# Strassen's scheme for the gate and value products of the last 832 tokens, with its weight sums made on the chip

## The chip, the cores and the metric

The kernel runs on one core of one Trainium2 chip. The metric is the device time of one execution in microseconds (us); the time of a kernel is the median of its runs. A profiled execution gives the trace; its span runs from the first instruction to the last.

## What is computed

Attention with a forget bias over 4 x 8 heads of 576 positions and head size 64, then a gated layer and a second layer, all in fp32:

```python
x = attention(q, k, v, s)                  # 2304 tokens x 512
g = x @ w_gate                             # 512 x 1536
x = (g * sigmoid(g) * (x @ w_val)) @ w_out # 1536 x 512
h = x @ w_in                               # 512 x 2048
out = (h * sigmoid(h)) @ w_out2            # 2048 x 512
```

## The kernel before

Every fp32 product is made of three matmuls: an operand is split into a high part that TensorE takes as fp32r and a low part (the rest), and high x high, high x low and low x high are added in PSUM. "Cutting" a tile means a copy on ScalarE that makes the high part and a subtraction, on POOL or VectorE, that makes the low part.

The first layer goes over three token groups of 576, 896 and 832 tokens (`SIZE`), called group zero, one and two here. Each group goes through the nine chunks of `L1`: two gate chunks, a down chunk, and so on three times. A gate chunk ("gv") holds 256 columns of the gate and of the value weights; `gate` makes, for each of two column blocks and each half of the tokens, two PSUM banks of 12 matmuls each, and `silu_mul` turns them into one tile of `h`. A down chunk ("o1") takes the last four tiles of `h`; `down` makes eight steps of 12 matmuls, and each is added into `acc` from PSUM. The weights of a chunk come in two loads of 1 MB (`w_half`, L416), the high and the low part side by side, asked for when the chunk before begins; `wt_p` has four such buffers, two chunks.

Attention runs beside group zero (its first units before it) and group one. The x of group two is written to DRAM as attention makes it and read back in the last chunk of group one (`x3_load`, `x3_cut`, L604 to L612).

The second layer (`up2`, `down2`) multiplies by Strassen's scheme in Winograd's form, with seven products in place of eight. Its weights need sums and cuts, which are prepared ahead, in 16 sets, beside the first layer. One set is: two loads of raw 64-bit weights, 512 KB each and in two DMAs (`ahead_load`, L457); their unpacking, two operations on ScalarE and two on VectorE for each load (`ahead`, `unpack`, L428 to L439); four sums on POOL (`u_sum`, L486); a cut of the weights themselves, 768 columns, and one of the sums, 1024 columns (`u_cut`, L497); and four stores to DRAM (`u_store`, L506). All these buffers come from `raw_p`, which has five. Eight sets are prepared beside group one, at every third or fourth quarter of a chunk, and eight beside group two, one in each of its first eight chunks. The x of the second layer's first 768 tokens is cut into its seven operands beside chunks one to seven of group two (`x2_sub`, `x2_cut`).

In group one the order on ScalarE, VectorE, POOL and SP comes from a planner that simulates the timeline, and only TensorE's is written by hand. From the last chunk of group one on (`last`, L949) every engine works in the order of the program: all queues are in order, SP, which issues the DMAs, among them. In that loop L991 to L1003 the functions of `more[n]` follow a quarter of a chunk's matmuls, stores of a set are put behind the next quarter's functions (`late`), and `after` holds the loads of the next set.

Of the kernel before, what the change touches and what calls it, by code (L numbers as in the profile page):

```python
# [33 lines left out]
BASE = [0, S, 2 * S + 320]  # L34
NG = len(SIZE)
# [38 lines left out]
def kernel(  # L74
# [13 lines left out]
    second_layer = ctx.enter_context(ExitStack())  # L88

# [314 lines left out]
    def w_load(c):  # L404
        wst[c] = []
        g = place[stream[c]]
        if first[c]:
            for e in range(CW // DW):
                t = raw_p.tile([P, DW, 2], U32, tag="wraw", name="r64")
                nc.sync.dma_start(out=t, in_=w64[g, :, e * DW : (e + 1) * DW, :])  # L410
                wst[c].append(t)
            return
        for e in range(2):
            w_half(c, e)
# [133 lines left out]
    def silu_mul(t, ph, hi, lo, n, pg, pv):  # L548
        u = tmp_p.tile([P, max(SIZE) // 2], F32, tag="u", name="u")[:, :n]
        if t == NG - 1:  # L550
            nc.scalar.activation(out=u, in_=pg[:, :n], func=AF.Silu)  # L551
        else:
            nc.scalar.activation(out=u, in_=pg[:, :n], func=AF.Tanh, scale=0.5)
            nc.vector.scalar_tensor_tensor(out=u, in0=u, scalar=1.0, in1=pg[:, :n], op0=ALU.add, op1=ALU.mult)  # L554
# [18 lines left out]
    def down(c, g, m, n0, n):  # L573
        b = batch[c]
        ps = ps_m.tile([P, 512], F32, tag="m", name="po")
# [28 lines left out]
    def x3_load(g):  # L604
        r = p2["x3", g] = raw_p.tile([P, SIZE[2]], F32, tag="wraw", name="x3r")
        nc.sync.dma_start(out=r, in_=x3_d[g])

    def x3_cut(g):
        r = p2.pop(("x3", g))
        x = xin[2][g] = p2["xt"].tile([P, 2, SIZE[2]], F32R, tag="x3", name="x3")  # L610
        copy("a", x[:, 0], r)
        nc.vector.tensor_tensor(out=x[:, 1], in0=r, in1=x[:, 0].bitcast(F32), op=ALU.subtract)  # L612

    def x2_load(t):
        for i in range(2):
            r = p2["x2", i] = p2["x2r"].tile([P, 2, 2, TN], F32, tag="x2r", name="x2r")
# [238 lines left out]
    def body():  # L855
# [47 lines left out]
        for q in range(8):  # L903
            x = 1 + 7 * q // 2
            for e in range(2):
                at_quarter(7 * (q - 1) // 2 + 2 if q else x - 4, lambda i=2 * q + e: ahead_load(i))
                at_quarter(x + e, lambda i=2 * q + e: ahead(i))
# [35 lines left out]
        p2["xt"] = pool("x3", NP, scope=first_layer)  # L943
        p2["x2"] = pool("x2", 10, scope=second_layer, side="right")
        p2["x2r"] = pool("x2r", 2, scope=second_layer, side="right")
        p2["ps"] = pool("ps_o", 4, PS, scope=second_layer, side="right")
        stores = []
        g = nc.gpsimd
        for c in range(last, n1):  # L949
            cur = chunk_steps(c)  # L950
            k = c - last - 1
            more = [[] for _ in range(4)]
            extra = []
            if k < 0:
                for x in range(NP):
                    more[0].append(lambda x=x: x3_load(x))
                    more[2 + x // 2].append(lambda x=x: x3_cut(x))
            if c + 1 < n1:
                more[0] += [lambda e=e: w_half(c + 1, e) for e in range(2)]
            q = 8 + k  # L960
            if 0 <= k < 8:
                more[0].append(lambda q=q: ahead(2 * q))
                more[1] += [lambda q=q: ahead(2 * q + 1), lambda q=q: u_sum(q)]
                for e in range(2):
                    more[2 + e].append(lambda q=q, k=e: u_cut(q, k))
                    more[2 + e].append(
                        lambda q=q, k=e: stores.extend(lambda e=e: u_store(q, k, e) for e in range(2))
                    )
            after = [[] for _ in range(4)]
            if k < 7:  # L970
                after[3].append(lambda i=2 * q + 2: ahead_load(i))
            if 0 <= k < 8:
                after[0].append(lambda i=2 * q + 1: ahead_load(i))
            if k == 0:
                more[2].append(lambda: x2_load(0))
            sub = {1: 1, 2: 2, 4: 3, 5: 4}.get(k)
            cuts = {1: [0], 2: [1], 3: [2, 3], 4: [4], 5: [5], 6: [6]}.get(k, [])
            if sub:
                more[0].append(lambda: x2_sub(0, sub))
            for e, x in enumerate(cuts):  # L980
                src = None if x in (0, 2, 5) else {1: 1, 3: 2, 4: 3, 6: 4}[x]
                f = lambda x=x, src=src: x2_cut(0, x, None if src is None else p2["t", src], g)
                if len(cur) == 4:
                    more[2].append(f)
                else:
                    extra.append(f)
            if k == 7:
                more[3].append(lambda: u_load(1, "Z"))
            if k == 8:
                more[0].append(lambda: u_load(0, "ZS"))  # L990
            for n, stp in enumerate(cur):  # L991
                if n == 0:
                    wst.pop(c - 1, None)
                stp()
                todo = more[n] if len(cur) == 4 else more[n // 2] if n % 2 == 0 else extra[n // 4 : n // 4 + n // 2 % 2]
                late, stores[:] = list(stores), []
                for f in todo:
# [106 lines left out]
```

## Time and profile before

| | |
|---|---|
| median of 3 runs | 1059.21 us (1057.55 to 1059.47) |
| profiled execution | 1057.37 us |
| its span | 1055.5 us |
| TensorE busy | 1010.6 us, 96% of the span |
| VectorE, ScalarE, POOL busy | 53%, 50%, 55% |
| mean granted TensorE clock | 0.983 |
| DMA | 254.87 MB, mean 241 GB/s |

The span has three parts that matter here: up to 492 us attention and the groups zero and one, to 699 us group two, and to the end the second layer. TensorE is the engine that is nearly always busy; matmuls are pipelined, so a row's time for one matmul is longer than the distance from one start to the next, and the rate is read from the starts. In rows, PE is TensorE, DVE is VectorE, ACT is ScalarE, SPq the queue that issues DMAs; L120 is the helper `copy`. The granted clock is a share of full speed. A line of windows ends with the mean granted clock, the DMA engines' busy share and GB/s.

### The profile page before, as it was taken

What the parts mean: (1) busy time and instruction counts of PE and PEld (TensorE: products, weight loads), DVE (VectorE), ACT (ScalarE), POOL (GpSimd) and SP (SyncE); (2) the same over time, 40 slices, a digit from 0 to 9 for tenths busy, and PEclk for the clock granted to TensorE, in tenths of its full rate; (3) what the DMA queues carried; (4) which work ended last, traced back from release to release, by engine and by line L of the source; (5) the groups of instructions that cost most, each with busy time, mean ns of one, the idle gap of its engine ahead of it and who ended that gap; (6) DMA issues with size and microseconds to landing.
All of it is one profiled execution on the core that took longest, in us unless ns stands there. A gap on an engine that the chain in (4) does not pass through costs nothing. (4 is left out here: it accounts for less than half of the span.)

```text
span 1055.5 us, 17759 instructions
## 1 busy us (share of the span) xinstructions
PE 1010.6 (96%) x6128; PEld 930.9 (88%) x6128; DVE 554.4 (53%) x1363; ACT 526.1 (50%) x1242; POOL 583.2 (55%) x729
## 2 busy tenths in 40 slices
PE   8999999999999999999978779799999999999998
PEld 7788878888888888889978769799999999999998
DVE  5877656655553554524211232236667666666556
ACT  6879877874475564422333423323345445443333
POOL 4766656553675776520444544534478555674445
PEclk9999999999999999999988989999999999999999
DMA  8479865888686855538755555699667977676663
GB/s 234 140 237 321 271 232 190 281 274 280 204 273 218 301 199 185 185 130 292 267 213 190 189 202 192 220 350 358 236 229 284 348 279 279 236 296 259 235 232 120
DMA packets 84138, 254.87 MB, mean 241 GB/s; under 512 B 10640, under 2 KB 33680, under 8 KB 70992
## 3 DMA queue, kind: packets, MB, share of 16 engines
q1 hardware_dynamic: 83904, 253.54, 67.7%
q8 instruction: 48, 0.79, 0.3%
q14 instruction: 42, 0.34, 0.1%
q10 hardware_dynamic: 144, 0.20, 0.1%
HBM read 194.26 MB, written 59.45 MB: 240 GB/s over the span
## 5 line engine op out<-in xcount | busy, mean ns | idle before, releaser
L672 POOL TENSOR_TENSOR h<-u,h 128x384 fp32r<-128x384 f32 x72 | 74.9, 1040 | 144.7 <-ACT h L120 137.1
L544 PE MATMUL pgv<-xt,wt 128*128 128x288 f32 (+1 forms) x384 | 131.5, 342 | 4.9 <-DVE u L554 4.9
L544 PE MATMUL po<-h,wt 128*128 128x288 f32 (+2 forms) x288 | 103.7, 360 | 27.2 <-ACT u L551 14.3
L557 POOL TENSOR_TENSOR h<-u,h 128x288 fp32r<-128x288 f32 (+2 forms) x72 | 74.0, 1029 | 99.0 <-ACT h L120 99.0
L545 PE MATMUL pgv<-xt,wt 128*128 128x288 f32 (+1 forms) x384 | 128.1, 334 | 0.0
L546 PE MATMUL pgv<-xt,wt 128*128 128x288 f32 (+1 forms) x384 | 127.9, 333 | 0.0
L120 ACT ACTIVATE h<-u 128x384 fp32r<-128x384 f32 (+3 forms) x144 | 75.0, 521 | 92.5 <-DVE u L555 91.6
L740 PE MATMUL po<-h,wt 128*128 128x384 f32 x336 | 112.5, 335 | 0.0
L741 PE MATMUL po<-h,wt 128*128 128x384 f32 x336 | 112.4, 335 | 0.0
L742 PE MATMUL po<-h,wt 128*128 128x384 f32 x336 | 112.4, 334 | 0.0
L695 PE MATMUL pu<-x,wt 128*128 128x384 f32 x330 | 111.8, 339 | 0.0
L698 PE MATMUL pu<-x,wt 128*128 128x384 f32 x330 | 111.8, 339 | 0.0
L699 PE MATMUL pu<-x,wt 128*128 128x384 f32 x330 | 111.8, 339 | 0.0
L672 POOL TENSOR_TENSOR h<-t,h 128x384 fp32r<-128x384 f32 x96 | 107.0, 1136 | 5.5 <-ACT h L120 5.5
L276 ACT ACTIVATE e<-e,m 64x64 f32<-64x64 f32 (+4 forms) x160 | 88.4, 553 | 34.6 <-DVE m L263 33.9
L545 PE MATMUL po<-h,wt 128*128 128x288 f32 (+2 forms) x288 | 101.1, 351 | 0.0
L546 PE MATMUL po<-h,wt 128*128 128x288 f32 (+2 forms) x288 | 100.6, 349 | 0.0
L701 ACT ACTIVATE s<-pu 128x384 f32<-128x384 f32 x48 | 23.6, 492 | 153.4 <-PE pu L699 153.4
L751 DVE TENSOR_TENSOR acc<-po,acc 128x384 f32<-128x384 f32 x144 | 76.8, 558 | 36.3 <-PE po L742 35.6
L124 POOL TENSOR_SCALAR e<-e,rl 128x128 f32<-128x128 f32 (+3 forms) x128 | 68.5, 548 | 43.2 <-DVE rl L288 41.9
L434 DVE SCALAR_TENSOR_TENSOR dk<-z,dk 128x512 uint32<-128x512 uint32 x32 | 26.8, 838 | 124.4 <-ACT dk L432 121.1
L544 PEld LDWEIGHTS po<-h,wt 128*128 128x128 f32 x288 | 57.1, 198 | 36.2 <-ACT u L551 15.3
(122 smaller groups left out, 2543.6 us busy)
## 6 DMA issues: line engine op xcount, KB each, us to landing
wt<-wu_d SPq DMA_DIRECT2D x48, 1024.0 KB, 8.6
wt<-w_d SPq DMA_DIRECT2D x36, 1024.0 KB, 7.4
wt<-wu_d SPq DMA_DIRECT2D x47, 768.0 KB, 5.9
r<-in_w_dram SPq DMA_DIRECT2D x36, 512.0 KB, 5.9
w_d<-wt SPq DMA_DIRECT2D x18, 1024.0 KB, 7.3
r<-in_w_dram SPq DMA_DIRECT2D x64, 256.0 KB, 4.9
qkr<-in_qk_dram SPq DMA_DIRECT2D x32, 288.0 KB, 5.3
cumb<-cum_d SPq DMA_DIRECT2D x15, 576.0 KB, 6.1
```

What stands on the lines that cost most here:

```text
L276: nc.scalar.activation(out=e[:r, hd, :wd], in_=e[:r, hd, :wd], func=AF.Exp, bias=m[hd][:r], scale=-1.0, accum_out=l[:r, hd : hd + 1],)
L544: nc.tensor.matmul(out=ps[:, :n], lhsT=a, rhs=xh, start=(k == 0), stop=False)
L545: nc.tensor.matmul(out=ps[:, :n], lhsT=a, rhs=xl, start=False, stop=False)
L546: nc.tensor.matmul(out=ps[:, :n], lhsT=c, rhs=xh, start=False, stop=(k == last))
L672: nc.gpsimd.tensor_tensor(out=h[:, 1], in0=u, in1=h[:, 0].bitcast(F32), op=ALU.subtract)
L695: nc.tensor.matmul(out=o, lhsT=a, rhs=x[:, 0, kk], start=fresh and kk == 0, stop=False, skip_group_check=True)
L698: nc.tensor.matmul(out=o, lhsT=a, rhs=x[:, 1, kk], stop=False, **more)
L699: nc.tensor.matmul(out=o, lhsT=c, rhs=x[:, 0, kk], stop=kk == 1, **more)
L740: nc.tensor.matmul(out=ps, lhsT=a, rhs=h[:, 0], start=fresh, stop=False, skip_group_check=True)
L741: nc.tensor.matmul(out=ps, lhsT=a, rhs=h[:, 1], stop=False, **more)
L742: nc.tensor.matmul(out=ps, lhsT=c, rhs=h[:, 0], stop=e == 1, **more)
L751: nc.vector.tensor_tensor(out=o, in0=ps, in1=o, op=ALU.add)
```

## The change

Group two's gate and value products go by the same seven-product scheme as the second layer: `up1` takes the place of `gate` there, over blocks of 256 features, 128 columns and `HN` = 416 tokens. For each chunk it makes seven products of six matmuls for the gate (`e` = 0) and seven for the value (`e` = 1), 84 matmuls of 416 columns. The products are added on VectorE, in PSUM or SBUF, the silu is taken by ScalarE from PSUM, and product, copy and low half give the tiles of `h`.

The sums of the weights are made beside the products, for each half chunk: `s_join` adds the high and low part of a weight load back together (1024 columns), `s_sum` makes four sums of 256, both on VectorE, and `s_cut` cuts them on ScalarE and POOL. The operands of x are cut by a new `x3_cut` from four differences (`x3_sub`), five of seven in the last chunk of group one.

Eleven sets are prepared beside group one in place of eight, three quarters of a chunk apart, from a quarter of the chunk ahead of it on. The other five go beside chunks two to six of group two. In these chunks the order is a table of positions: `fill[c, pos]` holds what follows product `pos` (of 14) of a gate chunk or step `pos` (of 8) of a down chunk. Down steps of group two take their PSUM banks from the pool `ps_o`, which also serves the unpacking. All seven cuts of the second layer's first x, and its first weight loads, move into the last down chunk.

```diff
 SIZE = [S, S + 320, 2 * S - 320]
+HN = SIZE[2] // 2
+NAHEAD = 11
...
     def down(c, g, m, n0, n):
         b = batch[c]
-        ps = ps_m.tile([P, 512], F32, tag="m", name="po")
+        if "ps" in p2:
+            ps = p2["ps"].tile([P, 512], F32, tag="o", name="po")
+        else:
+            ps = ps_m.tile([P, 512], F32, tag="m", name="po")
...
+    def x3_cut(i, eng):
+        x = p2["x3", "x", i] = p2["xm"].tile([P, 2, 2, HN], F32R, tag="x3", name="x3")
...
+        copy("a", x[:, 0], src)
+        eng.tensor_tensor(out=x[:, 1], in0=src, in1=x[:, 0].bitcast(F32), op=ALU.subtract)
+
+    def s_join(c, e):
+        z = p2["s", c, e, "z"] = p2["zs"].tile([P, CW // 2], F32, tag="zs", name="zs")
+        hi, lo = [x.bitcast(F32) for x in wst[c][e]]
+        nc.vector.tensor_tensor(out=z, in0=hi, in1=lo, op=ALU.add)
+
+    def s_sum(c, e):
...
+            nc.vector.tensor_tensor(out=o, in0=a, in1=b, op=op)
+
+    def s_cut(c, e):
+        r = p2["s", c, e, "r"]
+        t = p2["s", c, e] = p2["sp"].tile([P, 2, CW // 2], F32R, tag="sp", name="sp")
+        copy("a", t[:, 0], r)
+        nc.gpsimd.tensor_tensor(out=t[:, 1], in0=r, in1=t[:, 0].bitcast(F32), op=ALU.subtract)
+
+    def up1(c, e, fill):
...
+            u = g[j]
+            v.tensor_tensor(out=u, in0=x, in1=u, op=ALU.mult)
...
+            copy("a", hi, u)
+            nc.gpsimd.tensor_tensor(out=lo, in0=u, in1=hi.bitcast(F32), op=ALU.subtract)
+
+        for pos, (name, k, xi, bank) in enumerate(UP):
...
+            if xi in (0, 1):
+                y = ps["s", xi] = part(f"s{xi}")
+                nc.scalar.activation(out=y, in_=o, func=AF.Copy)
+            if xi == 3:
+                ps["w"] = part("w")
+                add(ps["w"], o, ps["s", 0])
+            if xi == 4:
+                add(o, o, ps["w"])
...
+                add(g[3] if e == 0 else ps["s", 1], o, ps["s", 1])
+            if xi == 2:
+                done(0, o)
+                done(3, g[3] if e == 0 else ps["s", 1])
+            if xi == 5:
+                add(o, o, ps["w"])
+                done(1, o)
+            if xi == 6:
+                done(2, o)
+            for f in fill.get((c, e * 7 + pos), []):
+                f()
...
-        for q in range(8):
-            x = 1 + 7 * q // 2
+        for q in range(NAHEAD):
+            x = 3 * q - 3
             for e in range(2):
-                at_quarter(7 * (q - 1) // 2 + 2 if q else x - 4, lambda i=2 * q + e: ahead_load(i))
+                at_quarter(x - 2, lambda i=2 * q + e: ahead_load(i))
...
+        def ahead_all(q, k, a0, a1, a2, a3, a4, a5, a6):
+            c = last + 1 + k
+            size = {"gv": 14, "o1": 8}
+            at(c - 1, size[stream[c - 1][0]] * 3 // 4, lambda: ahead_load(2 * q))
+            at(c, 0, lambda: ahead_load(2 * q + 1))
+            at(c, a0, lambda: ahead(2 * q))
+            at(c, a1, lambda: ahead(2 * q + 1))
+            at(c, a2, lambda: u_sum(q))
+            for k, pos in ((0, (a3, a4)), (1, (a5, a6))):
+                at(c, pos[0], lambda k=k: u_cut(q, k))
+                at(c, pos[1], *[lambda k=k, e=e: u_store(q, k, e) for e in range(2)])
...
+        for c in range(last, n1 - 1):
+            at(c, 0, *[lambda c=c, e=e: w_half(c + 1, e) for e in range(2)])
+        at(last, 2, lambda: x3_cut(0, g))
+        at(last, 3, lambda: x3_sub(1), lambda: x3_sub(2))
+        at(last, 4, lambda: x3_cut(3, v))
+        at(last, 5, lambda: x3_cut(1, g))
+        at(last, 6, lambda: x3_sub(3), lambda: x3_cut(4, v))
+        at(last, 7, lambda: x3_cut(2, g), lambda: x3_sub(4))
+        at(c0, 0, lambda: x3_cut(5, v))
+        at(c0, 1, lambda: x3_cut(6, g))
+        for c in range(c0, n1):
+            if stream[c][0] == "gv":
+                if c == c0:
+                    s_make(c, 0, last, 4, 5, 6)
+                elif stream[c - 1][0] == "gv":
+                    s_make(c, 0, c - 1, 7, 8, 9)
+                else:
+                    s_make(c, 0, c - 1, 4, 5, 6)
+                s_make(c, 1, c, 0, 1, 2)
+        for q in range(NAHEAD, 2 * NPR):
+            k = q - NAHEAD + 1
+            pos = (2, 6, 7, 9, 11, 11, 13) if stream[c0 + k][0] == "gv" else (1, 3, 4, 5, 6, 6, 7)
+            ahead_all(q, k, *pos)
+        at(c0 + 3, 0, lambda: x2_load(0))
...
+                at(c, 0, lambda: u_load(0, "ZS"), lambda: u_load(1, "Z"), sub(1), cut(0, g))
+                at(c, 1, sub(2), cut(3))
+                at(c, 2, cut(1, g))
+                at(c, 3, sub(3), cut(4))
+                at(c, 4, cut(2, g))
+                at(c, 5, sub(4), cut(5))
+                at(c, 6, cut(6, g))
```

## Rows read from the trace of the kernel before

**Rows 1.** Windows: us, then busy us (x instructions) of PE, PEld, DVE, ACT, POOL.

```profile
260.00:492.10 232.10, 232.10 (x1357) 196.46 (x1356) 110.18 (x302) 115.98 (x274) 128.98 (x180) 1.00 0.65 222
492.10:698.80 206.70, 176.06 (x865) 169.94 (x865) 47.99 (x77) 66.01 (x112) 94.10 (x79) 0.93 0.60 219
698.80:1055.50 356.70, 353.26 (x2018) 352.93 (x2016) 223.40 (x377) 150.24 (x326) 205.90 (x182) 1.00 0.69 265
```

**Rows 2.** Timeline of PE: start us, us, engine, line, operation, tiles.

```profile
252.60 0.37 PE L544 MATMUL pgv<-xt,wt 128*128 128x448 f32 x1
...
492.12 0.35 PE L544 MATMUL pgv<-x,wt 128*128 128x416 f32 x1
...
528.15 0.34 PE L546 MATMUL pgv<-x,wt 128*128 128x416 f32 x1
532.64 0.72 PE L544 MATMUL po<-h,wt 128*128 128x416 f32 x1 [4.14 <-ACT u L551]
...
538.95 0.35 PE L544 MATMUL po<-h,wt 128*128 128x416 f32 x1
```

**Rows 3.** Waits in group two: who for whom, us in total, times, longest.

```profile
PE po L544 <- ACT u L551: 14.3, 3, 5.8
...
ACT z L431 <- DMA r<-in_w_dram: 81.1, 15, 8.8
```

**Rows 4.** Timeline of SP's queue in group two: set loads (L473, L466), weight loads (L418).

```profile
495.40 1.07 SPq L473 DMA_DIRECT2D r<-in_w_dram  x2
...
641.45 1.01 SPq L418 DMA_DIRECT2D wt<-w_d  x2
642.56 0.90 SPq L473 DMA_DIRECT2D r<-in_w_dram  x2
...
667.01 1.34 SPq L466 DMA_DIRECT2D r<-in_w_dram  x2
```

**Rows 5.** Timeline of ACT: the unpack that waited for the load of 642.56.

```profile
652.81 0.66 ACT L431 ACTIVATE z<-r 128x512 f32<-128x512 f32 x1 [4.40 <-DMA r<-in_w_dram]
```

**Rows 6.** Timeline of POOL for the same set: first of four sums, low halves.

```profile
655.57 0.73 POOL L495 TENSOR_TENSOR s<-z 128x256 f32<-128x256 f32 x1 [6.00 <-DVE z L437]
...
659.51 1.85 POOL L503 TENSOR_TENSOR z<-z,cut 128x768 fp32r<-128x768 f32 x1
661.31 1.86 POOL L628 TENSOR_TENSOR x<-tt,x 128x768 fp32r<-128x768 f32 x1
...
664.16 2.40 POOL L503 TENSOR_TENSOR s<-s,cut 128x1024 fp32r<-128x1024 f32 x1
```

**Rows 7.** Groups by form in group two: count, busy us, mean ns, idle before.

```profile
L557 POOL TENSOR_TENSOR h<-u,h 128x416 fp32r<-128x416 f32 x24 | 26.1, 1089 | 53.8 <-ACT h L120 53.8
...
L555 DVE TENSOR_TENSOR u<-pgv,u 128x416 f32<-128x416 f32 x24 | 14.1, 588 | 38.3 <-PE pgv L546 22.1 <-ACT u L551 16.2
L120 ACT ACTIVATE h<-u 128x416 fp32r<-128x416 f32 x24 | 13.2, 552 | 34.1 <-DVE u L555 34.1
...
L586 DVE SCALAR_TENSOR_TENSOR acc<-po,acc 128x416 f32<-128x416 f32 x16 | 9.1, 588 | 14.5 <-PE po L546 14.3
```

**Rows 8.** Timeline of SP's queue in group one: loads of three sets.

```profile
260.24 2.80 SPq L466 DMA_DIRECT2D r<-in_w_dram  x4
...
295.37 2.69 SPq L473 DMA_DIRECT2D r<-in_w_dram  x4
...
314.05 5.99 SPq L466 DMA_DIRECT2D r<-in_w_dram  x4
```

**Rows 9.** Group by form: a subtraction of 832 elements on DVE.

```profile
L612 DVE TENSOR_TENSOR x<-x3r,x 128x832 fp32r<-128x832 f32 x4 | 3.9, 1017 | 0.0
```

**Rows 10.** Tile t of the second layer: count, ns min/median/max, first and last start.

```profile
L672 POOL TENSOR_TENSOR h<-t,h x96: 1002/1022/1344, 708.5 to 1044.5; 128x384 fp32r<-128x384 f32 x96
L677 DVE TENSOR_TENSOR t<-u,t x48: 810/925/1194, 707.4 to 1039.6; 128x384 f32<-128x384 f32 x48
...
L720 DVE TENSOR_TENSOR t<-u,pu x24: 543/544/546, 707.0 to 1038.1; 128x384 f32<-128x384 f32 x24
```

## Prediction: what the change does to the time

> **What bounds the kernel now.** I read the stages first: one line for the stretch from token group one's own chunks to its end, one for group two, one for the second layer [rows 1]. TensorE is busy all of the first stretch and nearly all of the last at the full clock; group two is the exception, 176.06 of 206.7 us busy at a mean clock of 0.93. So 30.6 us of idle time lie in the very stage that the change rewrites, and more time is lost to the low clock level.
>
> Next, how fast TensorE could go there. The 192 gate and value matmuls of the first two chunks start at 492.12 and the last of them at 528.15 [rows 2]: 36.03 us over 191 intervals, 0.1886 us each. The stage has 576 of these and 288 in the three down chunks: 864 x 0.1886 = 162.9 us against 206.7, 43.8 us lost. The same rows show how it is lost: 4.14 us of idle before the first down matmul, and then 18 matmuls from 532.64 to 538.95, 0.35 us each, which is the 1.2 GHz level; at the other level they would take 3.4 us, so 2.9 us more go.
>
> Then who is waited for. TensorE waits for ScalarE's silu, and ScalarE itself waits 81.1 us, 15 times, for one kind of transfer: the raw second-layer weights that the sets prepare ahead [rows 3]. ScalarE works in order, so an unpack whose data has not landed holds the silu behind it. The sync queue shows why the data is late. The last load of a set goes out at 495.40 for the first set and at 667.01 for the eighth [rows 4]: 171.61 / 7 = 24.5 us a set, while a chunk needs 96 x 0.1886 = 18.1 us. **The sets, not the matmuls, pace eight of the nine chunks.** One turn of that loop: landed 652.81 [rows 5], sums start 655.57, first low half 659.51, an x2 low half 661.31, second low half 664.16 to 666.56 [rows 6]; then its store, and at once the next load at 667.01 [rows 4]. That is 14.2 us to the load, and 10.25 us from the load at 642.56 to its landing at 652.81.
>
> **Part by part.**
>
> *Fewer products.* Seven of eight: per chunk 2 x 42 = 84 matmuls for 96, 72 fewer in six chunks, 72 x 0.1886 = 13.6 us of TensorE time; the stage's floor goes to 792 x 0.1886 = 149.4 us. It counts in full only in the chunks that no set paces: the first, and the fifth and sixth gate chunks.
>
> *Five sets instead of eight in group two*, in chunks two to six of nine. The loop's turn is built again. Landing to sums 2.8 us, the four sums 2.9, first low half 1.85, second 2.4. The x2 low half (1.86) leaves; in a gate chunk two low halves of h at 1.09 each [rows 7] come between: 12.1 us. On the sync queue the store now goes first, then the two weight loads, then the set's load. From the first weight load at 641.45 [rows 4] to the landing at 652.81 [rows 5] it is 11.36 us, and the store ahead of it adds 0.45 (666.56 to 667.01): 11.8 us. Turn: 23.9. In the down chunk a weight cut of 2.4 replaces the halves: 24.1, and I take 24.5 because its ScalarE part waits for a step's evacuation. In the third gate chunk the cut comes on top: 12.1 + 2.4 + some 1.2 for the join on VectorE ahead of it + 11.8 = 27.5. Four turns lie between the first and the fifth set: 24 + 24.5 + 27.5 + 24 = 100, plus 1.5 for operations of VectorE and POOL that hold each other up (below): 101.5. The queue's order matters: the store of a set's sums waits for POOL, and behind it wait both halves of the next chunk's weights, on SP and so on VectorE, which joins their two parts.
>
> *The sum.* First chunk from 492.1 to 507.9 (84 x 0.1886 = 15.8). The weight loads behind it wait for its buffers; the set's load follows 1.1 us later (641.45 to 642.56) and lands 10.25 after [rows 4, 5]: 519.2. Fifth landing 519.2 + 101.5 = 620.7. The down chunk beside it then has about four of eight steps left, 4 x 12 x 0.1886 = 9.1: 629.8. Two free gate chunks 31.7: 661.5. Before the last down chunk the final low half of h is late: product 0.59, copy 0.55, POOL 1.09 and one more in its queue 1.09 [rows 7], 3.3 in all, against 10 matmuls, 1.9, that need not wait: 1.4. The chunk itself 18.1: 681.0, where 698.8 stood. **17.8 us less.** The profiled execution took 1057.4 us, so 1039.6; it stands 1.8 below the median of the three runs, so about **1041** against 1059.2.
>
> *Three more sets in group one*: no TensorE work. Each brings 4 loads and 4 stores on SP, four unpacks, four decodes, four sums on POOL, two cuts. POOL takes 7.2 us a set: 21 us more on 129 busy of 232 [rows 1]. Spacing falls from 23 to about 20 us (three quarters of a chunk; group one's 36 quarters take 492.1 - 252.6 = 239.5 us, [rows 2]). TensorE never idles there now, and a spacing of 18.7 us occurs, 295.37 to 314.05 [rows 8]. I take 0; the other end is rival C.
>
> *Preparing x*: five of seven cuts and four differences move into the down chunk ahead of group two, beside 96 matmuls of 448 columns, 19.5 us (18.1 x 448 / 416). A subtraction of 832 elements takes 1.02 on VectorE [rows 9]; POOL by its rows about 2. VectorE: four differences, two low halves, eight evacuations at 0.59 [rows 7], one join and its sums, some 14 us; POOL 8.4. The weights for the first sums must land, some 10 us after issue, then join 1.25 (1.02 x 1024 / 832), four quarter sums, copy and a POOL cut of 2.4; that ends within a microsecond or so of its use. 0, at worst 2. The second layer's cuts and its first weights move into the last down chunk: POOL 4 x 1.86, VectorE 7 x 1.02 at most and the evacuations, 12 us, within 18.1; 0, and if that cover went, up to 2.
>
> *The sums on the fly* have no row of their own. Each half chunk: one join of 1024 and four sums of 256 on VectorE, 2.5 us by the 832 row if alone. Then come eight 416-wide additions and four products at 0.59: 2 x 2.5 + 12 x 0.59 = 12.1 us of VectorE in a gate chunk of 15.8, and a set's decoding on top. What stretches it can be read in the second layer: the difference of two SBUF tiles takes 0.93 us in the median, the same shape with one operand in PSUM 0.54, and POOL's own operation reaches 1.34 where its median is 1.02 [rows 10]. Ends: nothing, or 0.38 for every one of the ten joins and sums in a chunk. Only those ahead of a set's sums are in the loop, five of them in two turns; I take 1.5 us in all.
>
> The Trainium skill (SBUF — State Buffer, "Who interferes with whom") says that a VectorE operation with two SBUF inputs and a GpSimd operation that reads SBUF contend, and that the second to issue is held until the first is done. The trace agrees in kind, but the longest case, 1.19 for 0.54, is less than a whole POOL operation of 1.02. The rule taken in full would hold a join behind a 2.4 us cut, and that is rival B's direction.
>
> **Rivals.**
>
> *A: the loop no longer paces the stage* (the earlier first load and a shorter POOL part let the unpack go through in time). Then 149.4, plus 1.4 before the last down chunk, two other such places with a set's cut in POOL's queue at about 5 each, and 2.9 of low clock after each: 149.4 + 1.4 + 10 + 5.8 = 166.6, 40 us less, 1019. For it: the first load of each set now leaves a quarter of a chunk ahead, and the 11.8 us from store to landing is the one step that is ordered anew and may come out shorter. Against it: the turn loses only the 1.86 us of the x2 low half. Chance 0.18.
>
> *B: VectorE and POOL hold each other up throughout.* Ten operations a chunk that stretch POOL by 0.33 (1.34 - 1.02) each: 3.3 us a turn, 13.2 in four: 1054.6. For it: POOL has 4 x 1.09 + 2 x 2.4 + 2.9 + 1.85 + 2.4 = 16.4 us of work in a 15.8 us gate chunk with a set. Against it: most of these operations fall outside the loop's POOL part. Chance 0.17.
>
> *C: slower, by group one.* One spacing of sets there was 35.1 us, the next 18.7 [rows 8]; the turn of [rows 4] took 24.5 with no attention beside it. If eleven sets cannot follow each other in less than 26 us on average, ten spacings are 10 x (26 - 20) = 60 us behind plan. The last store, planned 31 quarters into group one at 252.6 + 31 x 6.65 = 459, comes at 519, 27 us into group two; the staging buffers, ScalarE and SP work in order and hold up the first set and the first weights of group two by that: 1041.4 + 27 = 1068. It decides once the mean spacing passes about 25 us, where the lateness eats the 17.8. Against it: the 18.7, a ScalarE busy 116 of 232 us and a POOL hardly more. Chance 0.10.
>
> **How the numbers follow.** The forecast, 0.55: its own range is 1033 to 1050, two microseconds either way on the mean turn making 8. The range 1022 to 1054 leaves out rival C and most of A. About 0.2%, 2.1 us, is what a measurement can tell here. Faster: 0.55 + 0.18 + 0.12 of B = 0.85; the same: 0.05, from B; slower: 0.10, from C.
>
> **What would show it.** Group two should last near 189 us, with 504 products at 0.189 us; the last load of a set should go out every 24 to 28 us, five times; ScalarE should still wait for the raw weights; the last three chunks should run nearly without idle; group one should keep TensorE full and the second layer its 356.7 us. The prediction is wrong if the set's spacing falls under 21 us, if TensorE idles in group one, or if VectorE's joins become what TensorE waits for.

## The result and the profile after

The changed kernel took 1066.12 us (median of 4 runs, 1064.08 to 1067.23), the kernel before 1058.91 beside it: a ratio of 1.0068, 95% interval 1.0049 to 1.0086. It is 0.7% slower, where 1041 was forecast. The profiled execution took 1065.69 us, its span 1063.9.

The windows of the changed kernel, by the same three stages as [rows 1]:

```profile
260.00:493.80 233.80, 232.30 (x1358) 196.45 (x1357) 124.24 (x310) 122.67 (x285) 149.29 (x195) 1.00 0.74 252
493.80:707.20 213.40, 171.72 (x794) 163.15 (x793) 131.50 (x179) 81.91 (x134) 112.57 (x72) 0.89 0.49 177
707.20:1063.90 356.70, 353.24 (x2017) 352.91 (x2016) 223.36 (x377) 150.30 (x326) 206.05 (x182) 1.00 0.71 263
```

Group one ends 1.7 us later, the second layer has its 356.7 us again; the loss is all in group two, 213.4 us for 206.7. Its products need 792 x 0.1886 = 149.4. So 64 us are lost: 213.4 - 171.7 = 41.7 idle, and 171.7 - 149.4 = 22.3 in matmuls that took longer than 0.1886, most of it at the lower clock level. (A matmul right behind a wait overlaps with none before it, which is 0.35 - 0.19 = 0.16 us for each of 15 waits, an estimate of 2.4 of the 22.3.) VectorE went from 48 to 131.5 us busy.

Whom TensorE waits for, in the whole span (us in total, times, longest):

```profile
PE pu L697 <- DVE g L665: 18.6, 5, 7.1
PE po L549 <- POOL h L681: 9.9, 4, 4.5
PE pu L701 <- POOL sp L659: 6.1, 3, 2.6
...
PE pu L697 <- ACT sp L123: 3.6, 2, 3.3
PE pu L697 <- DVE s L665: 3.5, 1, 3.5
```

and, of ScalarE's waits, the one that was 81.1 us in [rows 3]:

```profile
ACT z L435 <- DMA r<-in_w_dram: 15.3, 3, 11.5
```

So the raw weights of the sets are late only 3 times now, where it was 15. TensorE's waits have moved to VectorE's product additions (L665), POOL's low halves (L681) and the cuts of the new sums (L659). On SP's queue the last load of a set still goes out slowly (first, second and fifth set; [rows 4] answer to these):

```profile
521.90 0.90 SPq L470 DMA_DIRECT2D r<-in_w_dram  x2
...
550.47 1.40 SPq L477 DMA_DIRECT2D r<-in_w_dram  x2
...
631.11 1.28 SPq L470 DMA_DIRECT2D r<-in_w_dram  x2
```

That is (631.11 - 521.90) / 4 = 27.3 us a set. Whether the sets now hold up the chunks or the chunks the sets, these rows do not tell; the experiments go into it.

What the joins (zs) and sums (zr) cost, from the tiles' view (count, ns min/median/max, first and last start):

```profile
L641 DVE TENSOR_TENSOR zs<-wt x12: 1207/1535/3019, 490.0 to 672.2; 128x1024 f32<-128x1024 f32 x12
L653 DVE TENSOR_TENSOR zr<-zs x24: 406/438/1278, 493.4 to 676.1; 128x256 f32<-128x256 f32 x24
L653 DVE TENSOR_TENSOR zr<-zr,zs x12: 425/630/2509, 493.9 to 675.0; 128x256 f32<-128x256 f32 x12
L653 DVE TENSOR_TENSOR zr<-zs,zr x12: 411/418/2061, 494.6 to 676.5; 128x256 f32<-128x256 f32 x12
```

The shortest are near what the forecast assumed (1.21 for a join where it had 1.25, 0.41 for a sum where a quarter of 1.25 is 0.31); the longest are 2.5 to 6 times the shortest. The longest wait of TensorE, 7.13 us, can be followed back through all engines (timelines of VectorE, POOL, ScalarE and TensorE: start, us):

```profile
601.86 1.20 DVE L653 TENSOR_TENSOR zr<-zs 128x256 f32<-128x256 f32 x1
603.09 2.51 DVE L653 TENSOR_TENSOR zr<-zr,zs 128x256 f32<-128x256 f32 x1
605.52 1.28 DVE L653 TENSOR_TENSOR zr<-zs 128x256 f32<-128x256 f32 x1
606.72 1.28 DVE L653 TENSOR_TENSOR zr<-zs,zr 128x256 f32<-128x256 f32 x1
610.19 0.69 DVE L438 SCALAR_TENSOR_TENSOR dk<-z,dk 128x512 uint32<-128x512 uint32 x1 [2.19 <-ACT dk L436]
...
602.73 2.58 POOL L507 TENSOR_TENSOR s<-s,cut 128x1024 fp32r<-128x1024 f32 x1
605.27 2.45 POOL L681 TENSOR_TENSOR h<-g,h 128x416 fp32r<-128x416 f32 x2
...
608.03 1.06 ACT L123 ACTIVATE sp<-zr 128x1024 fp32r<-128x1024 f32 x1 [5.09 <-DVE zr L653]
609.00 0.65 ACT L435 ACTIVATE z<-r 128x512 f32<-128x512 f32 x1
...
612.92 0.72 PE L697 MATMUL pu<-x,wt 128*128 128x416 f32 x1 [7.13 <-DVE g L665]
```

Four sums of 0.42 us took from 601.86 to 608.0, 6.1 us, each of them ending 0.3 us after one of POOL's operations beside it (the cut of 602.73 ends at 605.31, the sum of 603.09 at 605.60). ScalarE's copy of the sums came 5.09 us late for it, the unpack of a set stands behind that copy, VectorE's decoding waited 2.19 for the unpack, and behind the decoding stood the additions whose banks TensorE needed. And then the restart is at the lower level of TensorE's clock (the window behind it, columns as above):

```profile
612.90:617.20 4.30, 4.28 (x12) 4.14 (x13) 0.47 (x1) 1.84 (x4) 0.00 (x0) 0.50 0.84 316
```

A granted clock of 0.50 (1.2 GHz) for 4.3 us after that wait, 12 matmuls in 4.3 us that take 12 x 0.1886 = 2.3 at the other level.

### The profile page after: what moved, and what is told of

It reads as the page before. It is cut to its first block, busy times and chain, and to the rows that moved or that the text cites. A ratio compares the mean times of both kernels' runs of the same rounds, so it can differ in the third digit from the quotient of the medians.

```text
span 1063.9 us, 17823 instructions
## 1 busy us (share of the span) xinstructions
PE 1006.4 (95%) x6056; PEld 924.0 (87%) x6056; DVE 654.1 (61%) x1477; ACT 552.0 (52%) x1281; POOL 627.1 (59%) x742
## 5 line engine op out<-in xcount | busy, mean ns | idle before, releaser
L549 PE MATMUL po<-h,wt 128*128 128x288 f32 (+2 forms) x288 | 99.1, 344 | 9.9 <-POOL h L681 9.9
L548 PE MATMUL po<-h,wt 128*128 128x288 f32 (+2 forms) x288 | 100.0, 347 | 0.0
L550 PE MATMUL po<-h,wt 128*128 128x288 f32 (+2 forms) x288 | 98.5, 342 | 0.0
L123 ACT ACTIVATE h<-u 128x384 fp32r<-128x384 f32 (+2 forms) x120 | 61.7, 514 | 55.6 <-DVE u L556 54.7
L548 PEld LDWEIGHTS pgv<-xt,wt 128*128 128x128 f32 x384 | 72.9, 190 | 18.1 <-issue 8.0
L438 DVE SCALAR_TENSOR_TENSOR dk<-z,dk 128x512 uint32<-128x512 uint32 x32 | 33.3, 1048 | 76.7 <-ACT dk L436 46.5
L549 PEld LDWEIGHTS pgv<-xt,wt 128*128 128x128 f32 x384 | 73.0, 190 | 3.4 <-DVE xt L393 0.3
```

Source lines behind the costliest of these rows:

```text
L548: nc.tensor.matmul(out=ps[:, :n], lhsT=a, rhs=xh, start=(k == 0), stop=False)
L549: nc.tensor.matmul(out=ps[:, :n], lhsT=a, rhs=xl, start=False, stop=False)
L550: nc.tensor.matmul(out=ps[:, :n], lhsT=c, rhs=xh, start=False, stop=(k == last))
```

## The experiments

Theory H: operations of VectorE with two SBUF operands and GpSimd's (POOL's) operations hold each other up, and in VectorE's order that delays the additions. Its rival L: the loop of the sets is the pace, as forecast, and turns more slowly.

**One part at a time.** First the sums were taken out, then the five sets; then came the kernel before with nothing but eleven sets ahead.

*Without joins and sums* (products with sums take the first weight matrix's high part):

```diff
     def s_join(c, e):
...
-        nc.vector.tensor_tensor(out=z, in0=hi, in1=lo, op=ALU.add)
+        p2["s", c, e, "hi"] = wst[c][e][0].bitcast(F32)
 
     def s_sum(c, e):
...
-            nc.vector.tensor_tensor(out=o, in0=a, in1=b, op=op)
+            pass
 
     def s_cut(c, e):
-        r = p2["s", c, e, "r"]
+        r = p2["s", c, e, "hi"]
```

> The changed kernel without the joins and the four sums of the weights (the seven products use the high part of the weights in their place; the cut on ScalarE and POOL stays). Theory H (VectorE's two-SBUF-operand work is held up by POOL, and the product additions queue behind it): some 57 us of VectorE work in group two go and TensorE's waits for VectorE with them; group two falls from 213.4 to about 175 to 185 us, the kernel to 1027 to 1037 us. Rival L (the loop of set loads, POOL and stores paces the chunks, as predicted): the spacing of the sets stays at 24 us or more, group two 200 us or more, the kernel at least 1052 us.

Measured: 1042.16 us (2 runs), ratio 0.9838 (0.9809 to 0.9867). Between the two ranges: the sums are worth 24 us, not all. The sets' second loads went out at 514.83 for the first and 614.42 for the fifth, 24.9 us a set. Where in group two the 24 us lie, the windows of its parts show: the first chunk, the five chunks with a set, the two free gate chunks; first of the changed kernel, then of this run.

```profile
493.85:521.33 27.48, 20.48 (x86) 18.77 (x85) 24.03 (x29) 12.00 (x17) 12.34 (x5) 0.81 0.43 159
521.33:649.04 127.71, 98.61 (x446) 93.84 (x445) 70.69 (x96) 47.32 (x81) 70.02 (x51) 0.87 0.51 185
649.04:687.33 38.29, 34.15 (x169) 32.64 (x169) 25.30 (x41) 16.06 (x27) 19.33 (x11) 0.96 0.41 148
```

```profile
495.78:514.22 18.44, 16.62 (x85) 15.50 (x84) 12.95 (x13) 11.53 (x17) 12.91 (x6) 1.00 0.58 213
514.22:633.64 119.42, 96.63 (x445) 90.65 (x445) 40.87 (x67) 49.13 (x83) 64.44 (x51) 0.90 0.55 201
633.64:665.38 31.74, 31.74 (x169) 31.46 (x169) 14.35 (x24) 14.05 (x25) 15.38 (x10) 1.00 0.46 166
```

The sums cost 9.0 us in the first chunk, 8.3 in the five with a set and 6.6 in the two free ones: 15.6 of 23.9 where no set stands.

*Without the five sets* (the second layer takes earlier ones again):

```diff
-            src = wu_d[steps[i][1], "ZSCE".index(name), :, :, :wide]
+            src = wu_d[steps[i][1] % 5, "ZSCE".index(name), :, :, :wide]
...
-        for q in range(NAHEAD, 2 * NPR):
+        for q in []:
```

> The changed kernel without the five sets beside group two (the second layer reads the earlier sets in their place). Rival L: nothing paces the chunks but TensorE, group two falls to about 155 us, the kernel to about 1008 us. Theory H: POOL loses some 40 of its 113 us and VectorE 14 of 132, but the joins and sums are still held up by POOL's low halves of h and of the weights, as in the first and fifth gate chunk of the changed kernel, which have no set and still lost 10 and 5 us: group two about 175 to 190 us, the kernel 1028 to 1042 us.

Measured: 1025.19 us (2 runs), ratio 0.9678 (0.9654 to 0.9701), a little under the range for H. With no set at all the stage still takes 170.7 us, 21 over its products, and a join has a mean of 1.92 us.

*Eleven sets ahead, eight products* (the kernel before; the other five sets in a row, beside the first five chunks of group two):

```diff
+NAHEAD = 11
...
-        for q in range(8):
-            x = 1 + 7 * q // 2
+        for q in range(NAHEAD):
+            x = 3 * q - 3
...
-            q = 8 + k
-            if 0 <= k < 8:
+            q = NAHEAD + k
+            if 0 <= k < 2 * NPR - NAHEAD:
...
```

> The kernel before with eleven sets beside group one and five beside group two, in its first five chunks, and with its eight products. Both theories: group one as in the changed kernel, some 1.7 us longer than before. The five chunks with a set keep the 24.5 us of a turn, the other four run near 18.1: 5 x 24.5 + 4 x 18.1 = 195 against 206.7 us, the kernel about 1047 to 1051 us.

Measured: 1042.28 us (1039.19 to 1044.57), ratio 0.9837 (0.9809 to 0.9865), better than expected. So of the change's two halves one gains 16.7 us, and what comes on top of it (seven products, their sums, the sets one chunk later, the second layer's first x cut in the last chunk) costs 1066.1 - 1042.3 = 23.8.

*The same with the five sets spread over group two:*

```diff
+AT = [0, 2, 4, 6, 7]
...
-            q = NAHEAD + k
-            if 0 <= k < 2 * NPR - NAHEAD:
+            q = NAHEAD + AT.index(k) if k in AT else 0
+            if k in AT:
...
```

> As the kernel with eleven sets ahead and eight products, but the five sets stand beside chunks one, three, five, seven and eight of group two, so that all but the last have two chunks' time, 36 us, for a turn of 24.5. If the turn alone slowed group two before, little is lost now: 163 us of TensorE work and under 10 of waits, the kernel 1024 to 1030 us. If a set beside a chunk costs its stall wherever it stands, five of the eight stalls stay: as with the sets in a row, about 1047 us.

Measured: **1017.17 us** (1015.45 to 1017.68), ratio 0.9597 (0.9577 to 0.9617), better than either kernel and than expected. Its stage, in the windows:

```profile
496.16:658.91 162.75, 162.75 (x865) 161.43 (x864) 41.81 (x65) 54.74 (x94) 74.89 (x61) 1.00 0.62 223
```

TensorE is busy all the time at the full clock: eight products, 864 matmuls, and nothing lost. Given room, the set loop hides entirely behind eight products. What is left over is group one, which ends at 496.16, 4.0 us later than before.

*Neither sums nor sets*: the edits of the first two runs together.

> The changed kernel without joins and sums and without the five sets that it prepares in group two. Left out are the sums of the weights (the products with sums take the first matrix's high part) and the second layer's last five sets (it takes earlier ones again). The sums alone gave 24 us and the sets alone 41. If the two delays add up, the stage falls by about 65 us to its products' 149 to 153 us and the kernel to 1000 to 1008. If they partly cover the same time, the stage stays at 155 to 165 and the kernel at 1010 to 1020. If something else in the change (the differences of x, the join of the scheme's results) has its own price, the first gate chunk alone stays at 20 us or more with neither.

Measured: 1011.74 us, ratio 0.9573 (0.9556 to 0.9591): the two delays partly cover the same time. The first chunk took 19.8, just under the 20 that would have pointed to something else in the change, and 4.0 over its products. The stages of the four corners, in the windows of the runs without sums, without sets, and without either:

```profile
495.78:685.27 189.49, 163.45 (x793) 155.50 (x792) 79.61 (x118) 81.24 (x134) 103.62 (x72) 0.94 0.54 197
...
496.33:667.02 170.69, 154.79 (x793) 149.58 (x792) 108.81 (x157) 62.48 (x104) 72.47 (x42) 0.98 0.38 136
...
494.23:653.57 159.34, 152.92 (x793) 149.24 (x792) 66.00 (x98) 61.70 (x104) 67.75 (x42) 0.99 0.40 143
```

The sums cost 213.4 - 189.5 = 23.9 us beside sets and 170.7 - 159.3 = 11.4 without; the sets 42.7 beside sums and 30.2 without. Each makes the other dearer by 12.5. With neither, the scheme's stage is only 3.4 us shorter than eight products with spread sets.

**Is it the reads of SBUF?** The same operations, but each with its second operand from a PSUM bank of zeros (left out: the low part in the join, the second matrix in the sums; the down steps have three banks in place of four):

```diff
-        nc.vector.tensor_tensor(out=z, in0=hi, in1=lo, op=ALU.add)
+        two = lambda x: x.rearrange("p (o n) -> p o n", o=2)
+        pc = p2["pc"].rearrange("p (o n) -> p o n", o=1).to_broadcast([P, 2, 512])
+        nc.vector.tensor_tensor(out=two(z), in0=two(hi), in1=pc, op=ALU.add)
...
+            b = p2["pc"][:, : 2 * P].rearrange("p (k m) -> p k m", k=2)
             nc.vector.tensor_tensor(out=o, in0=a, in1=b, op=op)
...
```

> The changed kernel, but in each join and each sum of weights VectorE takes its second operand from a PSUM bank of zeros in place of SBUF: as many operations of the same size on the same engine in the same order, and only one operand read from SBUF. Left out are the low part in the join and the second weight matrix in each sum; the cuts into three and all products stay. The down steps turn over three PSUM banks in place of four until the last down chunk. Theory H (VectorE's operations with two SBUF operands are held by GpSimd's while both read SBUF, and in VectorE's order of work that delays decoding and additions): joins fall to 1.2 to 1.5 us from 1.88, sums to 0.45 to 0.6 from 0.65 to 0.83, and the time comes to 1039 to 1050, near the kernel without sums (1042). Rival W (it is the added VectorE work and its place in the order, whatever it reads): joins and sums keep their means within 0.15 us, time 1058 to 1070.

Measured: 1049.67 us, ratio 0.9931 (0.9911 to 0.995), in H's range. The tiles' view of this run:

```profile
L643 DVE TENSOR_TENSOR zs<-wt,pc x12: 1208/1210/1221, 491.5 to 657.1; 128x1024 f32<-128x1024 f32 x12
L656 DVE TENSOR_TENSOR zr<-zs,pc x36: 403/412/420, 493.2 to 659.8; 128x256 f32<-128x256 f32 x36
L656 DVE TENSOR_TENSOR zr<-zr,pc x12: 420/421/423, 493.6 to 659.1; 128x256 f32<-128x256 f32 x12
```

Every operation now takes its shortest time, with POOL busy for the same share, 103.5 of 194.7 us (112.6 of 213.4 in the changed kernel). 1066.1 - 1049.7 = 16.5 of the sums' 24 us are the hold between VectorE and POOL; the other 7.5 go with VectorE's own time for them (and with the missing fourth bank, which was not priced by itself). The Trainium skill (SBUF — State Buffer, "Who interferes with whom") says that two SBUF inputs on VectorE and a GpSimd operation that reads SBUF block each other for a whole operation, and that outside the two-port modes a VectorE instruction with at most one SBUF input does not contend. The trace agrees in both halves, 2.51 us for a sum of 0.42 beside a cut of 2.58, and 0.42 at most with one operand in PSUM.

**Do other places for the sets help?** The changed kernel with its sets beside chunks two, four, six, eight and nine, then at the places of the 1017 us run; there also without sums, and with the PSUM operand:

```diff
-            k = q - NAHEAD + 1
+            k = (1, 3, 5, 7, 8)[q - NAHEAD]
```

> The changed kernel with the same five sets placed beside the second, fourth, sixth, eighth and ninth chunk of group two in place of five in a row; nothing is left out. With eight products this placing was worth 25 us (1042 to 1017). Theory H (VectorE held up by GpSimd) says that the sums stay dear wherever a set stands: no less than the 1025 of the kernel with no sets at all, 1028 to 1045. Theory S (the row of sets, its turn of 25 to 27 us, was all that failed): 1015 to 1025, at or below eight products with spread sets.

> The changed kernel with its five sets beside the first, third, fifth, seventh and eighth chunk of group two, the places that gave eight products 1017 us; nothing is left out. It ends a set one chunk earlier than the run with sets at the second, fourth, sixth, eighth and ninth chunk, whose last set came 3.8 us late for the second layer. Theory H (GpSimd's and VectorE's reads of SBUF hold each other up wherever a set stands beside sums): 1045 to 1065. Theory S (only the row, or only the late last set, was the trouble): 1015 to 1030.

> The same places without joins and sums (left out: the products with sums take the first weight matrix's high part). With the sets in a row this was 1042 us, its chunks with a set paced at 25 us. If that pace was the set's own loop, the places free it: 1012 to 1025. If a set's work beside the scheme's additions costs by itself, wherever it stands, 1030 to 1042.

> The same places, with each join and sum taking its second operand from a PSUM bank of zeros (left out: the low part in the join, the second matrix in each sum). Theory H: within 10 us above the run without sums at the same places, and at least 20 below the one with true sums there. Rival W (VectorE's time and order, not what it reads): within 10 us of the one with true sums.

Measured, in this order: 1067.19 us (1.0078 to 1.0124 of before), 1070.90 (1.0103 to 1.0147), 1041.47 (0.9819 to 0.9888), 1055.44 (0.9954 to 0.9988). Theory S falls, and so does the pace of the loop as the sole cause: places worth 25 us with eight products are worth nothing with seven, with or without sums, and the run without sums lies in the range for a set that costs by itself. That is a net figure: without sums, chunks three to six are 21 us shorter at these places (the third 19.9 us in place of 26.4, the fifth 19.6 in place of 27.8), but the last two, with sets beside the seventh and the eighth, rise from 15.9 and 19.9 to 23.8 and 27.0. Places without such a pair near the end were not run. The first two runs are even above H's ranges. In the first of them the last set's data came 3.8 us late for the second layer:

```profile
PE pu L809 <- DMA wt<-wu_d: 3.8, 1, 3.8
```

The PSUM operand gives 15.5 us back here, as before, but 14 stay above the run without sums, so it meets neither range: hold and VectorE's own time have about equal shares at these places. The run without sums at these places shows what a set does in VectorE's order (timelines of ScalarE and VectorE):

```profile
640.88 0.67 ACT L435 ACTIVATE z<-r 128x512 f32<-128x512 f32 x1 [2.13 <-POOL s L507]
...
642.10 0.70 DVE L438 SCALAR_TENSOR_TENSOR dk<-z,dk 128x512 uint32<-128x512 uint32 x1 [4.07 <-ACT dk L436]
642.88 0.69 DVE L441 SCALAR_TENSOR_TENSOR z<-r,dk 128x512 uint32<-128x512 uint32 x1
643.49 0.59 DVE L665 TENSOR_TENSOR pu<-pu,w 128x416 f32<-128x416 f32 x1
```

The unpack waits for POOL's last cut of the set before, the decoding for the unpack, the additions for the decoding.

**What of a set costs?** First the decoding on VectorE is left out for the five sets (their values are not put together), with sums and without:

```diff
-        unpack(z, wst.pop(("r", i)), k)
+        unpack(z, wst.pop(("r", i)), k, "av" if i < 2 * NAHEAD else "a")
```

> The changed kernel; left out are the two VectorE operations that finish each half of the decoding of the five sets of group two (20 operations of 0.69 us, 13.8 us in all); ScalarE still unpacks, GpSimd still sums and cuts. Theory Q (VectorE runs in order, and a decoding that waits for ScalarE's unpacking, up to 7 us, keeps the product additions behind it from TensorE): far more than 13.8 us comes back with the sums' price left: 1040 to 1052. Rival P (the sets cost through GpSimd's order, lows of h behind a set's cuts, and through the transfers): 1056 to 1066.

> The same left out of the kernel without joins and sums (there the products with sums take the first weight matrix's high part), which took 1042 us, and 1012 without sets at all. Theory Q: most of the 30 us between them come back, 1012 to 1026. Rival P: 1032 to 1042.

Measured: 1051.72 us (ratio 0.9946, 0.9923 to 0.9969) and 1034.95 (0.9784, 0.9749 to 0.9819). 14.4 and 7.2 us come back for 13.8 us of VectorE work: at the edge of theory Q's range in one, in rival P's in the other, and nowhere far more than the work itself. Q falls as the main cause. Without sums and decoding, the wait for a set's raw weights holds ScalarE, and TensorE behind it (timelines of ScalarE and TensorE):

```profile
596.39 0.66 ACT L435 ACTIVATE z<-r 128x512 f32<-128x512 f32 x1 [8.78 <-DMA r<-in_w_dram]
...
598.05 0.72 PE L697 MATMUL pu<-x,wt 128*128 128x416 f32 x1 [5.32 <-ACT s L704]
```

Then more room for the sets in that kernel (neither sums nor decoding, the places of the 1017 us run), and GpSimd's work for the five sets left out (their sums and the low parts of their cuts), without the new sums and with them:

```diff
     def u_sum(q):
...
+        if q >= NAHEAD:
+            return
...
     def u_cut(q, k):
...
-        nc.gpsimd.tensor_tensor(out=src.bitcast(F32R), in0=src, in1=hi.bitcast(F32), op=ALU.subtract)
+        if q < NAHEAD:
+            nc.gpsimd.tensor_tensor(out=src.bitcast(F32R), in0=src, in1=hi.bitcast(F32), op=ALU.subtract)
```

> No joins, no sums, no decoding of the five sets on VectorE (left out: the products with sums take the first weight matrix's high part, the five sets' values are not put together), sets beside the first, third, fifth, seventh and eighth chunk. In a row this took 1035 us, its chunks with a set again about 25 us apart. If the set's own loop is the pace, more room between the sets gives most of the 23 us down to the run with neither back: 1013 to 1024. If GpSimd's order costs in each place: 1028 to 1036.

> No joins and sums, and no GpSimd work for the five sets in a row (left out: their sums and their cuts' low parts; loads, unpacking, decoding, ScalarE's cuts and all stores stay; the products with sums take the first weight matrix's high part). Against 1042 with that work. GpSimd's order as the cause: 1018 to 1028. The loop of loads, unpacking and stores as the pace: 1034 to 1042, sets still about 25 us apart.

> The changed kernel, its joins and sums whole, without the five sets' sums and cuts on GpSimd (left out: these alone). Against 1066, and 1025 without sets. If sets are dear beside the sums because GpSimd's reads of SBUF (7.4 us a set) hold VectorE's, half or more of the 41 us come back: 1030 to 1046, and the mean of a sum falls by over 0.1 us. If GpSimd's cuts of the sums themselves do the holding, 1052 to 1064.

Measured: 1031.79 us (0.9709 to 0.9763), 1022.38 (0.9631 to 0.9687) and 1042.80 (0.9823 to 0.987), each in the range for GpSimd. Room alone gives 3 us; GpSimd's work for the sets is worth 1042.2 - 1022.4 = 19.8 us without the new sums and 1066.1 - 1042.8 = 23.3 with them. In the run with room, GpSimd accounts for 12.8 of 16.6 us that TensorE waits in group two:

```profile
PE po L549 <- POOL h L681: 8.4, 3, 3.5
PE pu L701 <- POOL sp L659: 4.4, 4, 1.8
PE pu L697 <- ACT s L704: 3.8, 1, 3.8
```

In the changed kernel without GpSimd's work for the sets a sum's three forms fall from 0.65, 0.83 and 0.71 us in the mean to 0.47, 0.62 and 0.42, while a join stays at 1.94. The four longest joins there, 3.0 to 3.3 us, are held by work that the change itself brings to POOL: two stand beside cuts of the new sums, two beside cuts of x. One thing stays open: GpSimd's part is both a stretch of the set's own loop (the turn falls from 24.9 to 21.0 us when it is left out) and a row of operations ahead of what the chunk needs, and how the 20 us divide between the two was not told apart.

**The account.** Idle time of group two and TensorE's time beyond its products, from the windows (stage minus TensorE busy; busy minus the matmuls at 0.1886 us, which holds the lower clock level and the lost overlap at each wait):

| group two of | stage | idle | beyond the products |
|---|---|---|---|
| before [rows 1] | 206.7 | 30.6 | 13.1 |
| changed | 213.4 | 41.7 | 22.3 |
| without sums | 189.5 | 26.0 | 14.1 |
| without sets | 170.7 | 15.9 | 5.4 |
| with neither | 159.3 | 6.4 | 3.5 |
| eight products, sets spread | 162.75 | 0 | 0 |

## Why the prediction was wrong

**The step that failed is the term for the sums on the fly**, "Only those ahead of a set's sums are in the loop, five of them in two turns; I take 1.5 us in all". The sums measured 24 us: 16.5 for the hold between VectorE and POOL, 7.5 for VectorE's own time. The forecast charged them only to the set loop and put them at nothing elsewhere, because VectorE had room. By the windows above, 15.6 us of their price lie in three chunks that have no set, and 8.3 in the five that do. VectorE is busy 131.5 of 213.4 us and still TensorE waits 18.6 us for its additions: these stand in order behind held joins and sums and, beside a set, behind a decoding that waits for ScalarE. Room on an engine says nothing about who stands first in its queue.

**The price of one operation** was right in the mean and wrong as a bound. From the tiles' view and the means (a join 1.88; sums 0.65, 0.83 and 0.71) the 60 joins and sums took 22.3 us more than 60 of the shortest, 0.37 each, and the upper end was 0.38. This is partly luck: that row comes from the second layer, where the POOL operations beside are 1.0 us long and the difference of two SBUF tiles had 1.19 for 0.54 at most [rows 10]. In group two the POOL operations are cuts of 2.4 us, sums of 0.7 and low halves of 1.1; many joins and sums were not held at all, and one sum lost 2.1 us behind a cut. How long one is held goes by the neighbour's length, not by its own. I had the rule that says so beside the row, as rival B's direction, and took the row.

**The set loop** came out near its number: without sums the turn was 24.9 us (25 before the 1.5 was added) and the stage 189.5 us against 188.9 - 1.5 = 187.4. In the changed kernel the turn was 27.3, within the stated 24 to 28, but the raw weights were waited for 15.3 us only. The path is borne out in part: without sums the same sets further apart left ScalarE 3.4 us of such waits in place of 22.7 and shortened the middle chunks, but not the whole (1041.5 for 1042.2), and 19.8 us hang on POOL's work for the sets, as a stretch of the loop or ahead of the chunk. So the agreement of the stage is in part luck. What I missed as well is that the loop need not pace: in the kernel before it can be hidden whole by placing the five sets further apart, which is 25 us of the 42 that the best version gains.

**Fewer products**: 792 matmuls, as counted. But 13.6 us of TensorE time were bought with 83.5 us of VectorE time, holds included (48.0 to 131.5), and the kernel with neither sums nor sets keeps only 3.4 us of the 13.6 against eight products with all their sets.

**The first chunk** was put at 15.8 us and x's preparation at "0, at worst 2". By TensorE's timeline it took 27.5 (493.85 to 521.3), and 19.8 with neither sums nor sets: 1.8 of waiting for the first cut on POOL and 2.2 of low clock stay even then. The last difference of x and its cut were held as the joins were: 2.76 and 2.79 us on VectorE, where [rows 9] had 1.02. The **two free gate chunks**, 31.7 forecast, took 38.3, and 31.7 without sums, so the sums cost without a set too. The **last down chunk** took 19.9 against 19.5, its wait 1.44 against 1.4.

**Group one** cost 1.7 us (0.7 to 4.9 in the profiles of the other runs with eleven sets), with 1.5 us of idle TensorE, where 0 was forecast; the second layer cost nothing, as forecast. Rival C, the one case on the slower side, did not happen. **Rival B** named the hold, at 13.2 us where 16.5 were measured, but by another path, through POOL's part of the loop. POOL's operations were stretched by 9.0 us in the whole stage (112.6 us busy, 103.5 with the PSUM operand); what cost most was VectorE's order, so B's near number is in part luck. The 7.5 of VectorE's own time stood in no rival: the forecast's 1041 less its 1.5, plus 16.5 and 7.5, is 1063.5, and 1066.1 was measured. **Rival A**'s condition came about by halves (ScalarE waited for raw weights 3 times, for 15.3 us), but its time of 1019 did not, because other waits took their place.

The warning I gave at the end, that it is wrong if VectorE's joins become what TensorE waits for, is how it came out: through the additions behind them.

## What to carry to other kernels

Before adding VectorE operations with two SBUF operands beside a busy POOL, price the worst of them at the longest POOL operation that can stand next to it, look at what is queued behind it on VectorE and on the engines that wait for it, and do so in every stretch of the stage, also where the engine has room; if one operand can be in PSUM, the hold is gone. Before saving matmuls, see what the present matmuls reach when only the waits are removed: here moving the prepared sets gained 42 us with no new arithmetic. An idle TensorE costs more than its idle time, so count the slow restart too.

## What the runs showed of the hardware

- The hold is for a whole operation, and it repeats: a sum of 0.42 us took 2.51 beside a cut of 2.58, and a join of 1.21 took up to 3.02. With one operand in PSUM the spread of 12 joins was 1.208 to 1.221 us, of 48 sums 0.403 to 0.423, beside the same cuts.
- It goes both ways: in the changed kernel a sum on POOL that began at 563.83, 0.22 us after a join of 1.22, took 1.60 us where the others of 256 columns take 0.74.
- TensorE's clock takes its share of most longer waits. In the table the time beyond the products, the lost overlap at each wait included, is 34 to 55% of the idle time (5.4 on 15.9, 13.1 on 30.6, 22.3 on 41.7, 14.1 on 26.0, 3.5 on 6.4), and with no wait there is none. Not every wait brings it: without sets the granted clock stayed at 1.00 behind a wait of 2.6 us (543.75). It comes on top of a wait that an estimate counts.
